# Half tiles moved between full tiles, weight sums moved out of the branches, in an attention and mixture-of-experts kernel

## The chip, the cores and the metric

The kernel runs on one core of a Trainium2 chip, as one launch. The metric is the device time of that launch in microseconds (us). Four engines compute: TensorE (PE in the profile; PEld is its loading of weights), VectorE (DVE), ScalarE (ACT) and GpSimd (POOL). SyncE (SP) only starts transfers. Each engine has its own instruction stream, and a small sequencer of its own (PEldq, DVEq, POOLq in the rows) that handles waits, register loads and branches.

## The reference

```python
# attention, per batch and head: S = 576, D = 64, each row sees itself and the 63 rows before it
scores = where(mask, q @ k.T / sqrt(D), -1e9)
attn = softmax(scores)
x = (attn @ v).transpose(0, 2, 1, 3).reshape(4608, 512)
# experts: 8 of them, every row goes to one
logits = x @ w_gate
expert_idx = argmax(logits, axis=1)
gate_w = softmax(logits)[arange(N), expert_idx]
for e in range(8):                       # rows sorted by expert
    h = maximum(x_sorted[lo:hi] @ w1[e], 0.0)      # 512 -> 1024
    y_sorted[lo:hi] = h @ w2[e]                    # 1024 -> 512
y = gate_w[:, None] * y_sorted[inv_perm]
```

All of it is float32. There are 4608 rows.

## The kernel before, in words

The kernel has three stages. In the first (lines 77 to 400) a scheduler lays out the attention, which writes x to the scratch buffer `x_dram` and collects the routing logits. The second (lines 407 to 530) runs mostly on VectorE: it ranks every row within its expert and turns the rank into a slot, so that `perm_i` holds, for each slot, the row that lies there, and `gate_t` its gate weight. Slots are grouped in tiles of 256 rows (`TB`, two chunks of 128). It also counts, per expert, the chunks in use (`chunks_i`), whether that count is odd (`odds_i`) and the first tile (`starts_i`).

The third stage works on tiles in a hand-written order (`tc.manual_schedule`), expert after expert. A full tile (`body` with `full` true) forms `hidden` and `output` by a scheme with seven products of quarter matrices instead of eight (`x`, `y`, `z`, `w`, and so on are the products), for which sums and differences of the quarters must be formed first: of the rows (`xs`, by `sums_x`), of the hidden values (`hs`, by `left_sums`), and of the weights (`sums_w1`, `sums_w2`, four operations of 128 x 1024 each, on GpSimd). A half tile (an odd last chunk of 128 rows) takes plain products (`plain_hidden`, `plain_output`). In this run there are 19 full tiles and 2 half tiles: three full tiles in three experts, two in five, and a half tile in two of those five.

How many tiles an expert has is known on the chip alone, so each tile stands under a branch: `If(chunks > 1)`, then `If(chunks > 3)` with `If(chunks > 5)` and `If(chunks > 7)` and a loop nested in it, then `If(odds > 0)` for the half tile. A skipped block has a short block in its stead, in which each engine adds to its semaphores what the skipped block would have added; GpSimd also adds it for the skipped indirect transfers.

The order of a tile: `scatter(before)` writes the rows of the tile before to the output with two indirect transfers; GpSimd copies the gate weights; `hidden` runs on the transposed rows `xq`; `turn` transposes the next tile's rows `xg` on TensorE and ScalarE copies them to `xq`; `sums_x` forms `xs` from them on GpSimd; `gather` starts two indirect transfers for the rows of the tile after the next; `output` runs. The first two full tiles of an expert carry an `aside`: at their end GpSimd forms the weight sums of the next expert (`sums_w1` in the first, `sums_w2` in the second; where a tile is skipped, its Else does it). `load_w` starts the transfer of the next expert's weights when the expert begins; two sets of weights are held. All eight experts' counts are loaded into registers of every engine (`values_load`, lines 702 and 703) after the first tile was turned and before the first branch. The last tile's rows are written by a scatter of their own at the end (lines 740 and 741).

`output` keeps five accumulators in half banks of three PSUM tiles `yp`; the product of `hs[:, 2]` adds to the accumulator of `hs[:, 1]`, after VectorE read that one.

## Time and profile before

| what | value |
| --- | --- |
| median of 3 runs (lowest, highest) | 907.71 us (904.1, 911.31) |
| profiled execution | 902.84 us |
| its span, first to last instruction | 901.1 us |
| TensorE busy with matmuls | 790.0 us, 88% of the span |
| VectorE, ScalarE, GpSimd busy | 390.9, 238.1, 371.4 us |
| mean granted TensorE clock | 0.941 of full speed |

The profiled execution lies 1.74 us above its span, and 4.9 us below the median of the three runs. Busy time is a sum over the whole span; the stages have different limits, so the argument goes by stage.

### The profile page before, as it was taken

What the parts mean: (1) busy time and instruction counts of PE and PEld (TensorE: products, weight loads), DVE (VectorE), ACT (ScalarE), POOL (GpSimd) and SP (SyncE); (2) the same over time, 40 slices, a digit from 0 to 9 for tenths busy, and PEclk for the clock granted to TensorE, in tenths of its full rate; (3) what the DMA queues carried; (4) which work ended last, traced back from release to release, by engine and by line L of the source; (5) the groups of instructions that cost most, each with busy time, mean ns of one, the idle gap of its engine ahead of it and who ended that gap; (6) DMA issues with size and microseconds to landing.
All of it is one profiled execution on the core that took longest, in us unless ns stands there. A gap on an engine that the chain in (4) does not pass through costs nothing. (4 is left out here: it accounts for less than half of the span.)

```text
span 901.1 us, 17469 instructions
## 1 busy us (share of the span) xinstructions
PE 790.0 (88%) x6832; PEld 675.9 (75%) x6832; DVE 390.9 (43%) x707; ACT 238.1 (26%) x606; POOL 371.4 (41%) x402
## 2 busy tenths in 40 slices
PE   6999999998931599989979989979989979989991
PEld 5776776776611499979979989969969969979991
DVE  4665665765628025424424432435313424403331
ACT  4554554554500022112211222112202202212220
POOL 3111111415000336635637732675663656663330
PEclk9999999999975799999989998999999989999996
DMA  6668678784080101133151115134134042110101
GB/s 138 153 163 218 147 186 202 197 261 111 3 291 1 35 17 45 47 120 132 48 203 36 36 50 209 47 97 163 43 111 152 34 160 90 49 54 25 48 28 43
DMA packets 140461, 94.46 MB, mean 105 GB/s; under 512 B 118192, under 2 KB 118192, under 8 KB 140338
## 3 DMA queue, kind: packets, MB, share of 16 engines
q1 hardware_dynamic: 128274, 61.90, 24.6%
q0 software_dynamic: 7200, 21.51, 7.2%
q10 hardware_dynamic: 4864, 9.44, 3.0%
q8 instruction: 74, 1.21, 0.6%
q14 instruction: 49, 0.40, 0.1%
HBM read 73.94 MB, written 20.97 MB: 105 GB/s over the span
## 5 line engine op out<-in xcount | busy, mean ns | idle before, releaser
L597 PE MATMUL hp<-xs,s 128*128 128x128 f32 x912 | 111.6, 281 | 0.0
L597 PE MATMUL hp<-xq,w 128*128 128x128 f32 x608 | 84.5, 299 | 28.9 <-PEq L737 23.1
L597 PEld LDWEIGHTS hp<-xs,s 128*128 128x128 f32 x912 | 108.9, 198 | 0.0
L597 PEld LDWEIGHTS hp<-xq,w 128*128 128x128 f32 x608 | 81.5, 213 | 32.7 <-issue 32.1
L629 PE MATMUL yp<-s,hs 128*128 128x256 f32 x456 | 101.5, 379 | 0.0
L284 ACT ACTIVATE pr<-sc,mx 128x128 f32<-128x128 f32 x288 | 79.7, 375 | 66.4 <-DVE mx L281 53.4
L629 PEld LDWEIGHTS yp<-s,hs 128*128 128x128 f32 x456 | 86.6, 190 | 11.8
L120 POOL TENSOR_TENSOR xs<-xq 128x256 f32<-128x256 f32 x44 | 36.9, 839 | 125.7 <-ACT xq L582 125.7
L572 POOL DMA_INDIRECT out_dram<-y,at_s x44 | 44.4, 1009 | 91.8 <-DMA out_dram<-y,at_s 70.1
L120 POOL TENSOR_TENSOR s<-w 128x1024 f32<-128x1024 f32 x32 | 75.3, 2356 | 12.2 <-DMA w<-in_moe_w_dram 12.0
L629 PE MATMUL yp<-w,hq 128*128 128x256 f32 x304 | 71.9, 379 | 0.0
L606 DVE TENSOR_TENSOR part<-hp,part 128x512 f32<-128x512 f32 x19 | 13.1, 692 | 131.3 <-PE hp L597 131.3
L215 POOL COPY vb<-va 64x520 f32<-64x520 f32 x32 | 19.7, 617 | 122.0 <-DMA va<-in_v_dram 70.6
L281 DVE TENSOR_REDUCE mx<-sc 128x3 f32<-128x384 f32 x96 | 49.1, 553 | 41.6 <-PE sc L274 40.2
L636 DVE SCALAR_TENSOR_TENSOR party<-yp,gates,party 128x256 f32<-128x256 f32 x57 | 26.1, 477 | 83.8 <-PE yp L629 83.8
L629 PEld LDWEIGHTS yp<-w,hq 128*128 128x128 f32 x304 | 56.3, 190 | 6.9
L604 ACT COPY part<-hp 128x512 f32<-128x512 f32 x19 | 11.1, 587 | 183.4 <-PE hp L597 183.4
L563 POOL DMA_INDIRECT xg<-x_dram,at_g x46 | 45.5, 989 | 13.6 <-issue 7.0
L293 PEld LDWEIGHTS tr<-ident,pr 128*128 128x128 f32 x288 | 34.4, 144 | 20.1 <-ACT qT L237 8.3
L293 PE MATMUL tr<-ident,pr 128*128 128x128 f32 x288 | 49.3, 286 | 0.1
L653 DVE TENSOR_TENSOR hs<-hq,hs 128x512 f32<-128x512 f32 x19 | 49.0, 2578 | 0.0
L274 PE MATMUL sc<-kT,qT 64*64 64x128 f32 x1152 | 46.5, 285 | 0.2
(137 smaller groups left out, 1379.9 us busy)
## 6 DMA issues: line engine op xcount, KB each, us to landing
w<-in_moe_w_dram SPq DMA_DIRECT2D x16, 2048.0 KB, 11.4
qs<-in_q_dram SPq DMA_DIRECT2D x64, 128.0 KB, 3.1
ks<-in_k_dram SPq DMA_DIRECT2D x64, 128.0 KB, 3.1
va<-in_v_dram SPq DMA_DIRECT2D x64, 128.0 KB, 2.6
x_dram<-xs ACTq DMA_DIRECT2D x8, 1024.0 KB, 5.9
qs<-in_q_dram SPq DMA_DIRECT2D x32, 32.0 KB, 2.5
ks<-in_k_dram SPq DMA_DIRECT2D x32, 32.0 KB, 2.2
vb<-in_v_dram SPq DMA_DIRECT2D x32, 32.0 KB, 2.6
```

Of the source, the lines that this page charges most:

```text
L120: op()
L215: nc.gpsimd.tensor_copy(out=vb[0:D, i].rearrange("p j h d -> p (j h d)"), in_=va[D:P, i].rearrange("p j h d -> p (j h d)"),)
L274: nc.tensor.matmul(out_, lhsT=qT[rows, t, a * WINDOW : (a + 1) * WINDOW], rhs=rhs, start=False, stop=True, skip_group_check=True,)
L281: nc.vector.tensor_reduce(out=mx[:], in_=scs[h][:], axis=AX.X, op=ALU.max, negate=True)
L284: nc.scalar.activation(out=pr[:, m, :], in_=scs[h][:, m, :], func=AF.Exp, bias=mx[:, m : m + 1])
L293: nc.tensor.transpose(out=tr[:, m, :], in_=prs[h][:, m, :], identity=ident[:])
L563: G.indirect_dma_start(out=xg[c][:], out_offset=None, in_=x_dram[:, :], in_offset=bass.IndirectOffsetOnAxis(ap=at_g[:, c : c + 1], axis=0),)
L572: G.indirect_dma_start(out=out[:, :], out_offset=bass.IndirectOffsetOnAxis(ap=at_s[:, c : c + 1], axis=0), in_=ys[c][:], in_offset=None, b ...
L597: nc.tensor.matmul(acc[:, f, :], lhsT=a[:, g, f * P : (f + 1) * P], rhs=b[:, g, :], start=(first and f == 0 and g == 0), stop=(g == HG - 1 ...
L629: nc.tensor.matmul(acc, lhsT=a[:, f, :], rhs=b[:, f, :], start=(first and f == 0), stop=(f == HF - 1), skip_group_check=True,)
L636: onto = lambda out, acc, c, more: V.scalar_tensor_tensor(out=out, in0=acc, scalar=gates[:, c : c + 1], in1=more, op0=ALU.mult, op1=ALU.add)
L653: next(more)()
```

## The change

- The half tile of an expert is worked second, behind its first full tile, and no longer last. For this the slots of the later tiles move up by one tile where an expert has an odd chunk (`late`), `halves_i` holds the tile of the half, and the later tiles stand at `at + odd + t`.
- `sums_w1` of the next expert stands at the start of the expert, ahead of the first branch; `sums_w2` between the first full tile and the branch of the half tile. There is no `aside` and no Else.
- The counts of an expert are loaded by `counts`, one expert ahead, behind `sums_w2` of the expert before it; only those of expert 0 are loaded at the start.
- `sums_x` runs on VectorE, in `output` behind the four sums of `hs`, which now stand together at its head; a half tile has it ahead of `plain_output`.
- `output` uses a sixth half bank (`y2`), so the product of `hs[:, 2]` adds to nothing; VectorE takes one operation more.
- `scatter` stands at the end of its own tile, and the gate weights of the next tile are copied after it. The scatters are declared free of order among themselves. The scatter at the very end is gone.

The diff, cut to its lines:

```diff
@@ -87,7 +87,8 @@
...
-    starts_i = consts.tile([P, E + 1], I32, name="starts_i")
+    starts_i = consts.tile([P, E], I32, name="starts_i")
+    halves_i = consts.tile([P, E], I32, name="halves_i")
@@ -491,12 +492,21 @@
...
+        V.tensor_copy(out=starts_i[:], in_=start[:])
+        V.tensor_single_scalar(halves_i[:], tiles_i[:], 1, op=ALU.min)
+        V.tensor_tensor(out=halves_i[:], in0=halves_i[:], in1=starts_i[:], op=ALU.add)
...
-        V.memset(starts_i[:, 0:1], 0)
-        V.tensor_copy(out=starts_i[:, 1:], in_=cum[:])
+        odd = rt.tile([P, E], F32, name="odd")
+        V.tensor_scalar_mul(odd[:], odds_i[:], float(P))
+        late = rt.tile([P, E, NJ], F32, name="late")
+        V.scalar_tensor_tensor(
+            out=late[:], in0=rank[:], scalar=float(TB + P), in1=per_e(odd, NJ), op0=ALU.is_ge, op1=ALU.mult
+        )
...
+        V.tensor_tensor(out=rank[:], in0=rank[:], in1=late[:], op=ALU.add)
@@ -569,10 +579,12 @@
...
-                G.indirect_dma_start(
+                put = G.indirect_dma_start(
...
+                tc.declare_no_dep(put.ins, group="puts", reason="every token has one slot, so no row is written twice")
+                tc.add_to_no_dep_group("puts", put.ins)
@@ -582,7 +594,7 @@
...
-            form(right_sums(G, xs, xq[:, 0, 0], xq[:, 0, 1], xq[:, 1, 0], xq[:, 1, 1]))
+            form(right_sums(V, xs, xq[:, 0, 0], xq[:, 0, 1], xq[:, 1, 0], xq[:, 1, 1]))
@@ -622,7 +634,6 @@
...
-            more = left_sums(V, hs, a11, a12, a21, a22)
@@ -638,25 +649,24 @@
...
-            x2, w2 = (p[:, hi] for p in yps[0:2])
-            next(more)()
-            next(more)()
+            x2, w2, y2 = (p[:, hi] for p in yps)
+            form(left_sums(V, hs, a11, a12, a21, a22))
...
-            next(more)()
+            sums_x()
...
+            product(y2, hs[:, 2], t[:, 2])
...
-            next(more)()
+            onto(v3[:], y, 1, y1b[:])
+            onto(v3[:], y2, 1, v3[:])
...
-            onto(v2[:], w2, 0, v2[:])
-            product(y, hs[:, 2], t[:, 2], False)
-            onto(v3[:], y, 1, y1b[:])
...
+            onto(v2[:], w2, 0, v2[:])
@@ -683,62 +693,62 @@
...
-        def body(e, before, now, after, full, aside=()):
-            scatter(before)
-            G.tensor_copy(out=gates[:], in_=gate_t[:, now])
+        def body(e, after, now, nxt, full):
...
-            sums_x()
...
-            (output if full else plain_output)(e)
-            for op in aside:
-                op()
+            if full:
+                output(e)
+            else:
+                sums_x()
+                plain_output(e)
+            scatter(now)
+            G.tensor_copy(out=gates[:], in_=gate_t[:, nxt])
+        def counts(e):
+            return (
+                nc.values_load(chunks_i[0:1, e : e + 1], min_val=0, max_val=NT // P),
+                nc.values_load(odds_i[0:1, e : e + 1], min_val=0, max_val=1),
+                G.value_load(starts_i[0:1, e : e + 1], min_val=0, max_val=NTILE),
+            )
+        coming = counts(0)
...
+        G.tensor_copy(out=gates[:], in_=gate_t[:, slice(1, 2)])
...
-        chunks = [nc.values_load(chunks_i[0:1, e : e + 1], min_val=0, max_val=NT // P) for e in range(E)]
-        odds = [nc.values_load(odds_i[0:1, e : e + 1], min_val=0, max_val=1) for e in range(E)]
...
-            at = G.value_load(starts_i[0:1, e : e + 1], min_val=0, max_val=NTILE)
-            if 1 < e + 1 < E:
-                load_w(e + 1)
-            aside = [partial(sums_w1, e + 1), partial(sums_w2, e + 1)] if e + 1 < E else []
+            chunks, odd, at = coming
+            if e + 1 < E:
+                if e:
+                    load_w(e + 1)
+                sums_w1(e + 1)
...
-                return bass.ds(i * C, C), bass.ds(i + 1, 1), bass.ds((i + 3) * C, C)
-            def full(t):
-                body(e, *place(at + t), True, aside[t : t + 1])
-            def otherwise(cond, t):
-                if aside:
-                    with cond.Else():
-                        aside[t]()
-            with tc.If(chunks[e] > 1) as one:
-                full(0)
-            otherwise(one, 0)
-            with tc.If(chunks[e] > 3) as two:
-                full(1)
-                with tc.If(chunks[e] > 5):
-                    full(2)
-                    with tc.If(chunks[e] > 7):
-                        full(3)
+                return bass.ds((i + 3) * C, C), bass.ds((i + 1) * C, C), bass.ds(i + 2, 1)
+            with tc.If(chunks > 1):
+                body(e, *place(at), True)
+            if e + 1 < E:
+                sums_w2(e + 1)
+                coming = counts(e + 1)
+            with tc.If(odd > 0):
+                half = G.value_load(halves_i[0:1, e : e + 1], min_val=0, max_val=NTILE)
+                body(e, *place(half), False)
+            with tc.If(chunks > 3):
+                body(e, *place(at + odd + 1), True)
+                with tc.If(chunks > 5):
+                    body(e, *place(at + odd + 2), True)
+                    with tc.If(chunks > 7):
+                        body(e, *place(at + odd + 3), True)
...
-                            body(e, *place(at + i), True)
-            otherwise(two, 1)
-            with tc.If(odds[e] > 0):
-                nxt = G.value_load(starts_i[0:1, e + 1 : e + 2], min_val=1, max_val=NTILE)
-                body(e, *place(nxt - 1), False)
-        end = G.value_load(starts_i[0:1, E : E + 1], min_val=0, max_val=NTILE)
-        scatter(bass.ds(end * C, C))
+                            body(e, *place(at + odd + i), True)
```

The order in which instructions stand changes at three places of the third stage. The names are the program's: `hp` and `yp` are PSUM tiles of `hidden` and `output`, `s` the weight sums, `party` partial outputs in SBUF.

On TensorE, the end of expert 0's first full tile and what follows it, before:

```order
L629 MATMUL yp_4342<-s_1_4176,hs 128x256 x4
L629 MATMUL yp_4341<-s_1_4176,hs 128x256 x4
L629 MATMUL yp_4342<-s_1_4176,hs 128x256 x4
L629 MATMUL yp_4340<-w_1_4174,hs 128x256 x4
L724 UNCONDITIONAL_BRANCH x2
L727 COMPARE_AND_BRANCH
L597 MATMUL hp_4337<-xq,w_1_4173 128x128 x8
```

and after:

```order
L640 MATMUL yp_4347<-w_1_4175,hs 128x256 x4
L735 UNCONDITIONAL_BRANCH x2
L711 TENSOR_LOAD chunks_i
L712 TENSOR_LOAD odds_i
L740 COMPARE_AND_BRANCH
L679 MATMUL hp_4344<-xq,w_1_4174 128x128 x16
L679 MATMUL hp_4345<-xq,w_1_4174 128x128 x16
L593 MATMUL tp_4342<-ident,xg_4324 128x128 x4
L593 MATMUL tp_4343<-ident,xg_4325 128x128 x4
L691 MATMUL yp_4347<-w_1_4175,hq 128x512 x8
L740 UNCONDITIONAL_BRANCH x2
L743 COMPARE_AND_BRANCH
```

Two register loads and the half tile with its branch now stand between the first and the second full tile; they stood at the start of the stage and behind the nested tiles.

On GpSimd, from the gather of expert 0's first tile to its second tile, before:

```order
L563 DMA xg_4318<-x_dram,at_g 128x512
L120 TENSOR_TENSOR s_1_4175<-w_1_4173 128x1024
L120 TENSOR_TENSOR s_1_4175<-s_1_4175,w_1_4173 128x1024
L120 TENSOR_TENSOR s_1_4175<-w_1_4173 128x1024
L120 TENSOR_TENSOR s_1_4175<-w_1_4173,s_1_4175 128x1024
L724 UNCONDITIONAL_BRANCH
```

and after, from the scatter of the first tile to the branch of the half tile:

```order
L582 DMA out_dram<-y_4338,at_s 4608x512
L707 ISA
L707 COPY gates<-gate_t 128x3
L735 UNCONDITIONAL_BRANCH
L735 ISA
L735 UNCONDITIONAL_BRANCH
L121 TENSOR_TENSOR s_1_4177<-w_1_4175 128x1024
L121 TENSOR_TENSOR s_1_4177<-w_1_4175,s_1_4177 128x1024
L121 TENSOR_TENSOR s_1_4177<-w_1_4175 128x1024
L121 TENSOR_TENSOR s_1_4177<-s_1_4177,w_1_4175 128x1024
L711 TENSOR_LOAD chunks_i
L712 TENSOR_LOAD odds_i
```

The sums of `w1` left the end of the first tile; the sums of `w2` stand there now, behind the tile's own scatter, and the branch of the half tile comes behind them.

On VectorE, one `output`, before:

```order
L618 TENSOR_TENSOR hq<-hp_4339,part_4324 128x512
L642 TENSOR_TENSOR hs<-hq 128x512
L643 TENSOR_TENSOR hs<-hs,hq 128x512
L650 TENSOR_TENSOR hs<-hq 128x512
L636 SCALAR_TENSOR_TENSOR party_4328<-yp_4342,gates,party_4326 128x256
L653 TENSOR_TENSOR hs<-hq,hs 128x512
L636 SCALAR_TENSOR_TENSOR party_4328<-yp_4341,gates,party_4328 128x256
```

and after:

```order
L121 TENSOR_TENSOR hs<-hq 128x512
L121 TENSOR_TENSOR hs<-hs,hq 128x512
L121 TENSOR_TENSOR hs<-hq 128x512
L121 TENSOR_TENSOR hs<-hq,hs 128x512
L121 TENSOR_TENSOR xs<-xq 128x256
L121 TENSOR_TENSOR xs<-xq,xs 128x256
L121 TENSOR_TENSOR xs<-xq 128x256
L121 TENSOR_TENSOR xs<-xs,xq 128x256
L647 SCALAR_TENSOR_TENSOR party_4335<-yp_4349,gates,party_4333 128x256
```

The fourth sum of `hs` stood behind an operation that waits for a product; all four now come first, and the four of `xs` follow.

## Rows read from the trace of the kernel before

**Rows 1.** Stage by stage, the last two stretches (us, busy us per engine, PEclk, DMA):
```profile
314.40:882.90 568.50, 533.94 (x3520) 491.72 (x3520) 212.69 (x286) 106.14 (x198) 300.88 (x288) 0.97 0.24 82
882.90:901.10 18.20, 0.01 (x1) 0.00 (x0) 0.48 (x1) 0.00 (x0) 2.21 (x3) 0.59 0.07 28
```

**Rows 2.** Timeline of TensorE, the transposes of four tiles (start, duration, instruction):
```profile
355.53 1.04 PE L581 MATMUL tp<-ident,xg 128*128 128x128 f32 x8
...
381.69 1.04 PE L581 MATMUL tp<-ident,xg 128*128 128x128 f32 x8
...
844.32 1.04 PE L581 MATMUL tp<-ident,xg 128*128 128x128 f32 x8
...
869.78 1.04 PE L581 MATMUL tp<-ident,xg 128*128 128x128 f32 x8
```

**Rows 3.** Groups from 300 to 902 us (busy, mean ns, idle before, releasers):
```profile
L597 PE MATMUL hp<-xq,w 128*128 128x128 f32 x608 | 84.5, 299 | 28.9 <-PEq L737 23.1 <-issue 5.7
...
L629 PE MATMUL yp<-w,hs 128*128 128x256 f32 x152 | 37.0, 386 | 6.4 <-DVE hs L653 6.4
...
L669 PE MATMUL hp<-xq,w 128*128 128x128 f32 x128 | 16.4, 294 | 5.0 <-PEq L729 5.0
...
L642 DVE TENSOR_TENSOR hs<-hq 128x512 f32<-128x512 f32 x19 | 13.2, 692 | 13.2 <-ACT hq L619 13.2
```

**Rows 4.** Timeline of TensorE at the end of two experts' full tiles:
```profile
392.93 1.89 PE L629 MATMUL yp<-w,hs 128*128 128x256 f32 x8
398.27 0.98 PE L597 MATMUL hp<-xq,w 128*128 128x128 f32 x3 [3.45 <-PEq L737]
...
659.51 2.85 PE L669 MATMUL hp<-xq,w 128*128 128x128 f32 x17 [2.65 <-PEq L729]
```

**Rows 5.** TensorE's sequencer, by line (ns min/median/max, first and last start us):
```profile
L737 PEldq COMPARE_BRANCH  x10: 85/2378/2778, 395.4 to 884.3; - x10
...
L731 PEldq COMPARE_BRANCH  x6: 184/1892/4602, 391.0 to 884.1; - x6
...
L702 PEldq TENSOR_LOAD <-chunks_i x8: 300/306/499, 307.5 to 310.6; - x8
```

**Rows 6.** Ten microseconds behind each restart, first and last of seven (columns of Rows 1):
```profile
398.27:408.27 10.00, 10.00 (x76) 10.00 (x77) 1.38 (x2) 1.18 (x2) 1.47 (x3) 0.85 0.91 326
...
791.38:801.38 10.00, 10.00 (x77) 9.04 (x78) 0.69 (x1) 1.56 (x3) 3.62 (x5) 1.00 0.07 29
```

**Rows 7.** Timeline at the start of the third stage:
```profile
306.36 2.30 PE L581 MATMUL tp<-ident,xg 128*128 128x128 f32 x8 [4.86 <-DMA xg<-x_dram,at_g]
...
314.40 3.77 PE L597 MATMUL hp<-xq,w 128*128 128x128 f32 x16 [5.74 <-issue]
```

**Rows 8.** Timeline in the second tile of expert 0, VectorE beside GpSimd:
```profile
363.99 3.25 DVE L653 TENSOR_TENSOR hs<-hq,hs 128x512 f32<-128x512 f32 x1
364.32 2.36 POOL L120 TENSOR_TENSOR s<-w 128x1024 f32<-128x1024 f32 x1
366.76 2.70 POOL L120 TENSOR_TENSOR s<-w,s 128x1024 f32<-128x1024 f32 x1
```

**Rows 9.** Transfers and GpSimd's sequencer, by line (L137, L572, L737, L765):
```profile
DMA to landing us min/median/max: 8.0/8.7/11.5
...
DMA to landing us min/median/max: 2.1/2.7/8.1
...
L737 POOLq INC_SWDGE_SEM  x6: 482/962/1922, 395.1 to 884.7; - x6
...
L765 POOLq DRAIN  x3: 46/113/8672, 891.5 to 900.8; - x3
```

**Rows 10.** Timeline of the tail:
```profile
883.00 0.48 DVE L636 SCALAR_TENSOR_TENSOR y<-yp,gates,party 128x256 f32<-128x256 f32 x1 [0.32 <-issue]
...
888.77 1.02 POOL L572 DMA_INDIRECT out_dram<-y,at_s  x1 [0.71 <-POOL at_s L569]
891.77 1.00 POOL L572 DMA_INDIRECT out_dram<-y,at_s  x1 [1.97 <-DMA out_dram<-y,at_s]
```

## Prediction

> **What bounds the kernel now.** I read the windows by stage first. From the first hidden product at 314.40 us to 882.90 us TensorE computes in 533.9 of 568.5 us, while VectorE, ScalarE and GpSimd are each busy for little more than half of it or less; behind 882.90 lies a tail of 18.2 us in which hardly anything computes [rows 1]. So the third stage is TensorE's, and the question is what keeps TensorE from 34.6 us of work in it, what slows it, and what the start and the tail cost. The first stage keeps its order, so I take it as unchanged.
>
> The timeline gives a full tile's price without trouble: the transposes of two tiles in a row near the end, where no weight sums are formed any more, stand 25.46 us apart; in expert 0 they stand 26.16 us apart [rows 2]. The groups by line say who is waited for [rows 3]: 28.9 us ahead of the first products of `hidden`, 23.1 of them put down to TensorE's own sequencer at the branch of the half tile (L737) and 5.7 to the first start; 5.0 us ahead of a half tile, put down to the sequencer at L729; and 6.4 us ahead of products that wait for the fourth sum of `hs`. So 23.1 + 5.0 = 28.1 us fall at seven ends of a run of full tiles. One of them shows the pattern: the array ends at 394.82 and starts at 398.27, 3.45 us later; ahead of a half tile it is 2.65 us [rows 4], ahead of the other half tile 5.0 - 2.65 = 2.35. The sequencer's list says why [rows 5]: a branch over a block takes 2.4 us in the median at L737 and up to 4.6 us at L731. The first at L731 starts at 391.0, thus 3.8 us before the array ends. The sequencer runs that far ahead, so the first jump of an expert's end is mostly covered and the second isn't.
>
> The clock follows. [...] The sum of what is missing is 1.33 windows, 13.3 us. The one window with 1.00 stands behind the shortest gap, 2.35 us; the others follow 2.65 us and more.
>
> **The change part by part**, against the profiled execution of 902.84 us; the median of the runs, 907.71, lies 4.9 us above it, and I carry that over.
>
> *Start.* Sixteen register loads (two lists of eight, 0.44 us from one to the next [rows 5]) stand between the end of the transposes at 308.66 and the first product, 5.74 us [rows 7]. After, two loads of 0.3 us stand ahead of the transposes, beside their wait for the gather. The routing gains `odd`, `late` and a sum ahead of the slots: three operations that the trace lacks; at most 0.48 us each, as an operation of 128x256 takes [rows 10], and little over nothing for fewer columns. I take the dear end, since small operations pay mostly their start: 5.7 - 1.4 = **-4.3** (bounds -3 to -5.5).
>
> *Skips.* At an expert's end only the skip over the nested tiles is left, since the half tile's stands earlier; 2.4 to 4.6 us against a lead of 3.8 leaves 0 to 0.8. TensorE's next products also wait for the short blocks of the others, VectorE's above all, whose last operation ends 0.5 us behind the array. I take 1.0 at seven ends (0.85 to 1.6), and 0.9 once in the last expert. Behind the first full tile of the six experts without a half tile the sequencer has two loads and a jump: 0.9 + 2.4 to 4.6 - 3.8 = -0.5 to 1.7. VectorE's chain there is 0.48 + two loads of 0.3 + some 0.3 for its block, 1.4. I take 1.4 at five of them (up to 2.4; the sixth is the last expert's). The two experts with a half tile fall through. Sum 7.0 + 0.9 + 7.0 = 14.9 in place of 28.1: **-13.2** (bounds -16 to -4).
>
> *Clock.* All these gaps are below 2.35, behind which the clock stayed at 1.00, so the loss of **-13.3** goes. If the five behind first tiles come out at 2.65 or more, each pays what such a restart pays now, 13.3 / 6 = 2.2 us: -2.3 is the other bound.
>
> [...]
>
> *The fourth sum of `hs`.* In fourteen tiles it waits for an operation that waits for a product, and meets GpSimd's weight sums: 3.25 us where VectorE's like takes 0.69 [rows 3, 8]. Those tiles cost 26.16 - 25.46 = 0.70 us more: 14 x 0.70 = **-9.8**. With all four at the head nothing stands before them.
>
> *What GpSimd's sums meet now.* The sums of `w1` start when the weights land, 8.0 to 8.7 us after their issue at the expert's start [rows 9], and take four times some 2.4 us [rows 8]; they end some 18 us into the first tile, while the four sums of `hs` stand from 14 to 17 us and the second is wanted at about 19. That overlap did not exist before. If VectorE's four take 3.25 instead of 0.69 each, they end at 27 and the products wait some 2 us in each of six experts, or 11 us in all; if they meet only the last sum, nothing. I take 1.0 us in all (**+1.0**, bounds 0 to 11), as the second sum, which is wanted first, has some 3 us of slack, one operation of 3.25.
>
> *Sums of `w2` on GpSimd's queue.* They begin behind the first tile's scatter, and the short block for the skipped half tile stands behind them in GpSimd's queue. The scatter's two issues, of 1.0 us each [rows 10], lie about 1.4 to 3.7 us behind the tile's end; four sums of 2.4 us end at some 13.2 us, and the block's additions for skipped transfers take 0.5 to 1.9 us [rows 9]. Waiting for them is `turn` of the second tile, 14 us in. So it waits 0 to 1.4 us in five experts; I take 0.85 each: **+4.3** (bounds 0 to 7).
>
> *`xs` on VectorE, the sixth half bank.* Four sums of half the width of those of `hs` and one more operation of 0.48 us cost VectorE about 2 us in a tile of 25.5, in which it is busy for 10; they lie behind the sums that TensorE waits for. `xs` is wanted a tile later. Nothing on the path. Should VectorE run late, the next tile's first products would wait; I see no row for that.
>
> *Tail.* Now the last operation of `y` ends at 883.5, and the last scatter is issued at 888.77 and 891.77, the second behind a wait of 1.97 us; then GpSimd drains for up to 8.7 us [rows 9, 10]. After, the scatter stands in the tile, ahead of the closing branches, so some 4.5 us earlier, but its drain has the skipped blocks in front of it still. I take **-4.0** (bounds -1 to -6.6: the whole of 888.77 - 883.5 and the half of the wait that is not the first transfer's).
>
> **Sum**: -4.3 - 13.2 - 13.3 - 9.8 + 1.0 + 4.3 - 4.0 = -39.3. The profiled execution comes to 863.5, the median to 907.7 - 39.3 = **868 us**.
>
> **The rivals.** *The lead is lost behind the first tile.* It needs the sequencer to be 3.8 us ahead; a wait late in `output` would take that away. Then five gaps cost 3.8 in place of 1.4 and 2.2 of clock: 5 x 4.6 = +23, 891 us. For it speaks that the second of two jumps is uncovered now; against it, that the first is covered.
>
> *Slower: every skip is paid in idle array.* There are twelve of them (seven ends, five first tiles), where now seven gaps hold all. With a gap x and a clock loss of 2.2 at each, the sum gains 12 (x + 2.2) - 14.9: at 4.6 us, the longest jump, +66.7, thus 935 us. It breaks even at x = 2.3 us (908 us), and as the clock held behind 2.35 us, a gap just above that is where it decides. For it: skips that stood in pairs now stand alone, each with loads or waits before it. Against it: the lead of 3.8 at the end of a full tile [rows 4, 5] covers most of a single skip.
>
> [...] A sum of `hs` begun at 363.99 ended at 367.24, though GpSimd's sum began later, at 364.32 [rows 8]; so VectorE loses whichever begins first. If all sums of `hs` wait for the last of `w1`, the term of 1.0 becomes 11: 878 us. [...]
>
> *The change removes nothing.* That the idle time only moves is the break-even of the second rival, 908.
>
> **How the numbers follow.** The sum as it stands 0.72, the port 0.06, the lead lost at first tiles 0.10, every skip paid 0.12, of which 0.07 near the break-even and 0.05 above. One per cent, 9 us, is about what a measurement of this kernel tells from no change. So faster 0.88, same 0.07, slower 0.05. The sum's own bounds, with not all at one end, are 855 to 885; to hold 8 in 10 the range reaches to the lost lead: 855 to 892.
>
> **What would show it.** Idle time of TensorE behind first full tiles and at experts' ends near 1 to 1.4 us, and the clock at 1.00 behind them; transposes of full tiles 25.5 us apart with no wait for the fourth sum of `hs`; at second tiles a wait of `turn` for GpSimd of at most 1.4 us; the first hidden product near 310; a tail of some 14 us. I am wrong if gaps of 2.4 us and more stand at more than seven places, if `hs` of first tiles takes 3 us an operation and is waited for, or if `turn` waits for GpSimd for several microseconds.

## The result, and the profile after

The changed kernel takes 875.85 us (median of 4 runs, 875.18 to 876.66); the kernel before, beside it, 906.35 us (904.1 to 911.31). The ratio is 0.966, with an interval of 0.961 to 0.970: 30.5 us less, where 39.3 were forecast, and inside the range. The profiled execution has a span of 874.8 us, 26.3 us less than the span before.

The start, on TensorE's timeline of the changed kernel (start, duration, instruction, idle time before it):

```profile
311.47 1.08 PE L593 MATMUL tp<-ident,xg 128*128 128x128 f32 x4 [4.92 <-DMA xg<-x_dram,at_g]
...
313.77 3.62 PE L609 MATMUL hp<-xq,w 128*128 128x128 f32 x16
```

The first product stands 2.3 us behind the first transpose, before it was 8.0 [rows 7]; the 5.74 us of idle time are gone. Yet it starts only 0.6 us earlier, since the transposes start 5.1 us later. The copy that ends the first stage shows why, in VectorE's timeline of the kernel before and of the changed one:

```profile
256.44 0.23 DVE L367 COPY logits<-tr 128x72 f32<-128x72 f32 x1 [1.96 <-PE tr L363]
```

```profile
260.46 0.23 DVE L368 COPY logits<-tr 128x72 f32<-128x72 f32 x1 [1.96 <-PE tr L364]
```

So 4.0 us of the 5.1 were there before the routing began, in a stage whose instructions stand in the same order in both kernels. Most of that agrees with a lower granted clock: in windows of 15 us over the first 255 us, 5.1 us of full clock are missing in the profile before and 8.7 us in this one. The other 1.1 us are the routing's new operations, among them two of 128x288, 0.46 us each, and one of 128x8, 0.16 us: with 8 columns for 288 an operation still takes a third of the time.

What TensorE waits for in the third stage of the changed kernel (engine, line and releaser: us in all, times, the longest):

```profile
PE hp L609 <- DVEq L740: 6.4, 5, 1.4
PE yp L640 <- DVE hs L121: 4.7, 8, 0.8
PE hp L609 <- DVEq L745: 3.4, 4, 0.9
PE hp L609 <- issue: 2.5, 1, 2.5
PE tp L593 <- DMA xg<-x_dram,at_g: 2.0, 4, 1.0
PE hp L609 <- DVEq L747: 1.6, 2, 0.8
```

Against [rows 3] the 23.1 and 5.0 us put down to TensorE's own sequencer have gone. In their place stand gaps of 1.4 us behind first full tiles (L740 and, for one that ends at 343.58, 1.5; in the last expert, which loads no counts, 0.7) and of 0.8 to 0.9 at experts' ends (L745, L747), which VectorE's sequencer ends; with one of 2.5 us at an expert's end they come to 15.4 us at thirteen places, where there were 28.1 at seven. The wait for `hs` is a new one: not for the fourth sum, but in first tiles, for the earlier ones. The transposes' wait behind GpSimd, which the prediction has, is there with 2.0 us.

Windows of ten microseconds behind an expert's end and behind a first tile, and the tail (us, busy us per engine, granted clock of TensorE, DMA):

```profile
395.66:405.66 10.00, 10.00 (x89) 10.00 (x90) 2.08 (x3) 1.25 (x3) 2.22 (x3) 1.00 0.97 339
685.45:695.45 10.00, 10.00 (x89) 10.00 (x90) 2.08 (x3) 1.26 (x3) 9.62 (x7) 1.00 0.14 55
858.65:874.80 16.15, 0.00 (x0) 0.00 (x0) 0.48 (x1) 0.00 (x0) 2.22 (x3) 0.66 0.08 31
```

The granted clock is 1.00 in the ten microseconds behind each of the thirteen restarts; behind the same expert's end it was 0.85 before [rows 6]. Before, the five windows between the first and the last of [rows 6] lay below 1.00, too:

```profile
457.60:467.60 10.00, 10.00 (x67) 10.00 (x68) 0.81 (x2) 1.18 (x2) 1.21 (x2) 0.74 0.89 307
541.92:551.92 10.00, 10.00 (x63) 10.00 (x64) 0.69 (x1) 1.18 (x2) 1.46 (x3) 0.69 0.90 323
602.67:612.67 10.00, 10.00 (x75) 10.00 (x76) 1.38 (x2) 1.18 (x2) 1.21 (x2) 0.83 0.91 321
659.51:669.51 10.00, 10.00 (x73) 9.91 (x74) 0.69 (x1) 0.90 (x2) 4.34 (x5) 0.83 0.06 26
733.90:743.90 10.00, 10.00 (x67) 10.00 (x68) 0.72 (x2) 1.18 (x2) 1.21 (x2) 0.73 0.90 322
```

The tail is 2.0 us shorter, not 4.0.

A tile without weight sums beside `hs` has its price of 25.5 us: expert 0's second tile lies between these transposes, 25.49 us apart, where it took 26.16 before [rows 2].

```profile
356.22 1.06 PE L593 MATMUL tp<-ident,xg 128*128 128x128 f32 x8
...
381.71 1.04 PE L593 MATMUL tp<-ident,xg 128*128 128x128 f32 x8
```

First tiles of later experts are longer. The worst, on TensorE, and VectorE and GpSimd in it:

```profile
668.90 1.04 PE L593 MATMUL tp<-ident,xg 128*128 128x128 f32 x8
...
675.84 1.99 PE L640 MATMUL yp<-s,hs 128*128 128x256 f32 x8 [0.72 <-DVE hs L121]
678.60 3.72 PE L640 MATMUL yp<-s,hs 128*128 128x256 f32 x16 [0.76 <-DVE hs L121]
...
685.45 2.02 PE L609 MATMUL hp<-xq,w 128*128 128x128 f32 x16 [1.40 <-DVEq L740]
...
699.15 1.06 PE L593 MATMUL tp<-ident,xg 128*128 128x128 f32 x8 [0.97 <-DMA xg<-x_dram,at_g]
```

```profile
670.49 2.54 DVE L121 TENSOR_TENSOR hs<-hq 128x512 f32<-128x512 f32 x1 [0.69 <-ACT hq L631]
673.07 2.72 DVE L121 TENSOR_TENSOR hs<-hs,hq 128x512 f32<-128x512 f32 x1
675.71 2.83 DVE L121 TENSOR_TENSOR hs<-hq 128x512 f32<-128x512 f32 x1
678.47 0.68 DVE L121 TENSOR_TENSOR hs<-hq,hs 128x512 f32<-128x512 f32 x1
```

```profile
667.69 2.36 POOL L121 TENSOR_TENSOR s<-w 128x1024 f32<-128x1024 f32 x1 [8.25 <-DMA out_dram<-y,at_s]
...
672.43 2.80 POOL L121 TENSOR_TENSOR s<-w 128x1024 f32<-128x1024 f32 x1
675.20 2.79 POOL L121 TENSOR_TENSOR s<-w,s 128x1024 f32<-128x1024 f32 x1
```

Three of the four sums of `hs` take the time of a GpSimd sum each; only the last, behind GpSimd's end, takes 0.68 us. From transpose to transpose (668.90 to 699.15) it is 30.25 us; without the gap of 1.40 and the transposes' wait of 0.97 it is 27.88.

### The profile page after: what moved, and what is told of

It reads as the page before. It is cut to its first block, busy times and chain, and to the rows that moved or that the text cites. A ratio compares the mean times of both kernels' runs of the same rounds, so it can differ in the third digit from the quotient of the medians.

```text
span 874.8 us, 17497 instructions
## 1 busy us (share of the span) xinstructions
PE 780.4 (89%) x6832; PEld 664.8 (76%) x6832; DVE 430.0 (49%) x818; ACT 237.7 (27%) x606; POOL 307.7 (35%) x312
## 5 line engine op out<-in xcount | busy, mean ns | idle before, releaser
L609 PE MATMUL hp<-xs,s 128*128 128x128 f32 x912 | 108.4, 276 | 0.5 <-DVE part L618 0.5
L640 PE MATMUL yp<-s,hs 128*128 128x256 f32 x456 | 103.4, 381 | 4.7 <-DVE hs L121 4.7
L609 PEld LDWEIGHTS hp<-xs,s 128*128 128x128 f32 x912 | 105.3, 193 | 0.7 <-DVE part L618 0.7
L121 POOL TENSOR_TENSOR s<-w 128x1024 f32<-128x1024 f32 x32 | 78.3, 2449 | 57.2 <-DMA out_dram<-y,at_s 38.3
L609 PE MATMUL hp<-xq,w 128*128 128x128 f32 x608 | 76.6, 280 | 15.4 <-DVEq L740 7.9
L609 PEld LDWEIGHTS hp<-xq,w 128*128 128x128 f32 x608 | 73.0, 196 | 21.2 <-issue 21.0
L573 POOL DMA_INDIRECT xg<-x_dram,at_g x46 | 50.3, 1094 | 79.4 <-PE tp L593 69.1
L647 DVE SCALAR_TENSOR_TENSOR party<-yp,gates,party 128x256 f32<-128x256 f32 x76 | 34.9, 479 | 57.4 <-PE yp L640 56.2
L121 DVE TENSOR_TENSOR hs<-hq 128x512 f32<-128x512 f32 x38 | 45.2, 1190 | 13.2 <-ACT hq L631 13.2
L275 PEld LDWEIGHTS sc<-kT,qT 64*64 64x64 f32 x1152 | 33.9, 138 | 12.6 <-issue 8.6
```

The lines of the kernel that those rows point to most:

```text
L121: op()
L275: nc.tensor.matmul(out_, lhsT=qT[rows, t, a * WINDOW : (a + 1) * WINDOW], rhs=rhs, start=False, stop=True, skip_group_check=True,)
L573: G.indirect_dma_start(out=xg[c][:], out_offset=None, in_=x_dram[:, :], in_offset=bass.IndirectOffsetOnAxis(ap=at_g[:, c : c + 1], axis=0),)
L609: nc.tensor.matmul(acc[:, f, :], lhsT=a[:, g, f * P : (f + 1) * P], rhs=b[:, g, :], start=(first and f == 0 and g == 0), stop=(g == HG - 1 ...
L640: nc.tensor.matmul(acc, lhsT=a[:, f, :], rhs=b[:, f, :], start=(first and f == 0), stop=(f == HF - 1), skip_group_check=True,)
L647: onto = lambda out, acc, c, more: V.scalar_tensor_tensor(out=out, in0=acc, scalar=gates[:, c : c + 1], in1=more, op0=ALU.mult, op1=ALU.add)
```

## The experiments

Each changes one thing in the changed kernel (875.85 us) unless it says otherwise. They were timed in three groups, beside which the kernel before took 905.05, 908.15 and 907.83 us, so differences between groups of 2 us or less say little; the traces say more. The ratios are to the kernel before.

**The sums of w1 left out.** The sums of `w1` are formed for the second expert only.

```diff
-                sums_w1(e + 1)
+                if not e:
+                    sums_w1(e + 1)
```

> The changed kernel, but GpSimd forms the sums of w1 for the second expert only; experts 3 to 8 then work with old sums, so that part of the computation is left out. Theory A: in the first tiles of experts 2 to 7 the sums of hs take up to 2.8 us each beside these sums, and that costs the 7.5 us by which those tiles are longer than 25.7; with five of these six left undisturbed (the sums for expert 2 stand in the first expert's tile, where none was lengthened), the hs sums take 0.7 us, the idle time ahead of the products of hs (4.7 us) goes to nothing, and the time falls by 6 to 7.5 us to about 869. Theory B: these tiles are longer because the weight transfer or the restart after the branch makes the sums late; then the time stays within 1.5 us of 876 and the hs sums stay long.

Measured: 870.57 us (869.13 to 871.2), ratio 0.962 [0.958, 0.965]. (All six lengthened tiles were left undisturbed, not five, as the expectation has it.) VectorE's second sum of `hs` in the same tile as above, and TensorE there:

```profile
667.18 0.69 DVE L121 TENSOR_TENSOR hs<-hs,hq 128x512 f32<-128x512 f32 x1
```

```profile
664.87 1.04 PE L593 MATMUL tp<-ident,xg 128*128 128x128 f32 x8
...
679.39 2.02 PE L609 MATMUL hp<-xq,w 128*128 128x128 f32 x16 [1.40 <-DVEq L741]
...
693.12 1.07 PE L593 MATMUL tp<-ident,xg 128*128 128x128 f32 x8 [0.99 <-DMA xg<-x_dram,at_g]
```

The sums take 0.69 us, no product of `hs` waits, and the tile takes 28.25 - 1.40 - 0.99 = 25.86 us, 2.0 less. Theory A holds: GpSimd's sums of `w1` cost this, not the restart or the transfer. Over the six experts the same difference, tile by tile, comes to 7.2 us. The medians differ by 5.3; in the profiled execution one restart, at 581.97, loses clock (0.83 over ten microseconds, 1.7 us), which may be the rest.

**The sums of w1 in the first tile, behind its gather.**

```diff
             gather(after)
+            if aside:
+                aside()
...
-                sums_w1(e + 1)
...
+            if aside:
+                with one.Else():
+                    aside()
```

> The changed kernel with the sums of w1 back in the expert's first tile, behind its gather (an Else forms them where that tile is skipped). Theory A: the sums of hs run while GpSimd waits for the gather's turn, so at most the last of them meets a sum of w1; the 7.5 us in first tiles go. But GpSimd ends these sums 1 to 2 us behind the tile's end, so the sums of w2 and the short block end later, and the second tile's transposes wait 0.5 to 1 us more in five experts: in all 870 to 872 us. Theory B (the first tiles are long for another reason): 876 to 880.

Measured: 897.37 us (896.33 to 898.32), ratio 0.991 [0.988, 0.995], 21 us slower than the changed kernel and outside of both theories. TensorE's waits, VectorE behind `hs`, and TensorE's restart:

```profile
PE hp L609 <- DVEq L745: 28.9, 6, 5.7
```

```profile
417.94 2.57 DVE L121 TENSOR_TENSOR xs<-xq 128x256 f32<-128x256 f32 x1
```

```profile
429.99 2.26 PE L609 MATMUL hp<-xq,w 128*128 128x128 f32 x9 [5.64 <-DVEq L745]
```

No product waits for `hs` any more, but now it is `xs` that stands beside GpSimd's sums: three of its four operations take 2.5 us, for 0.42 elsewhere. VectorE ends its tile 4 us later, reaches its two branches later, and TensorE's gap behind the first tile grows from 1.4 to 5.6 us, with a lower clock behind it. That `xs` costs nothing, as the prediction had it, held in these runs only where GpSimd formed no sum beside it (0.42 us an operation).

**The sums of w2 behind the half tile's branch.**

```diff
-                sums_w2(e + 1)
                 coming = counts(e + 1)
...
+            if e + 1 < E:
+                sums_w2(e + 1)
             with tc.If(chunks > 3):
```

> The changed kernel with the sums of w2 behind the half tile's branch, not ahead of it. Theory A: the second tile's transposes wait (0.17 to 0.97 us, 2.0 us in all) because GpSimd's additions in the short block of the skipped half tile stand behind the sums of w2; with these behind the branch the waits go: -2.0 us, about 874. Rival: what they wait for is the rows' gather itself, or the sums that now stand closer to the second tile make its gather late: 876 or some us more.

Measured: 874.56 us (873.22 to 875.57), ratio 0.965 [0.962, 0.969]. The transposes that waited 0.97 us before them in the changed kernel, in this run's timeline:

```profile
698.31 1.04 PE L593 MATMUL tp<-ident,xg 128*128 128x128 f32 x8
```

No transpose of the third stage waits any more. In time it is 1.3 us, no more than groups differ by; the trace shows theory A's wait gone.

**The half tile last again.**

```diff
-        V.tensor_tensor(out=rank[:], in0=rank[:], in1=late[:], op=ALU.add)
...
+                            body(e, *place(at + i), True)
             with tc.If(odd > 0):
                 half = G.value_load(halves_i[0:1, e : e + 1], min_val=0, max_val=NTILE)
```

> The changed kernel with the half tile last in its expert again (slots and branch order as before, all else as changed). Theory A: the place of the half tile is what splits the pair of skips; with it back at the end, seven ends have gaps of 2.4 to 5.3 us again, those behind first tiles fall to 1 us or less, and behind each gap of 2.65 us or more the clock falls again: 28 us of gaps for 15 and some 13 us of clock, so about 893 to 902 us. Rival: the gaps became short because GpSimd's sums and the register loads moved; then 874 to 880 us and no window of the third stage below a clock of 1.00.

Measured: 881.41 us (878.74 to 883.36), ratio 0.973 [0.969, 0.977]. TensorE's largest wait, one window behind an expert's end, and the tail:

```profile
PE hp L601 <- PEq L741: 13.9, 4, 3.7
```

```profile
395.61:405.61 10.00, 10.00 (x75) 10.00 (x76) 1.38 (x2) 1.18 (x2) 0.63 (x2) 0.83 0.92 334
```

```profile
860.56:880.20 19.64, 0.00 (x1) 0.00 (x0) 0.48 (x1) 0.00 (x0) 2.22 (x3) 0.57 0.07 26
```

The pair of skips is back at four ends, 3.3 to 3.7 us each, but no gap is over 3.7 where the kernel before had three over 5.2, and the gaps ahead of half tiles, 2.4 and 2.6 us before, are 0.8 now. Behind first tiles there is none. So 5.6 us, not 17 to 26: both theories were off. In the trace the gaps come to 17.8 us for 15.4, so the place of the half tile bears little of what the skips gained. It bears more of the clock: behind five restarts the windows are at 0.71 to 0.83 and miss 9.7 us. The tail takes 3.5 us more. Against these stand waits that shrink, for `hs` from 4.7 to 1.3 us and of the transposes from 2.0 us to none. Something else had made the remaining skips shorter; the next run shows what.

**The fourth sum of hs late again.**

```diff
-            form(left_sums(V, hs, a11, a12, a21, a22))
+            more = left_sums(V, hs, a11, a12, a21, a22)
+            for _ in range(3):
+                next(more)()
...
             onto(v2[:], y, 0, y1a[:])
+            next(more)()
```

> The changed kernel with the fourth sum of hs behind the first operation on the accumulators again, all else as changed. Theory A, as the prediction had it: its place behind a wait is what cost 0.70 us in fourteen tiles, so some 10 us come back, 884 to 887 us. Theory B: the loss came from GpSimd's sums standing beside it, which the change moved to the start of the first two tiles; then the sum takes 0.7 us, TensorE doesn't wait for it, and the time stays at 875 to 877. Theory C: TensorE doesn't wait, but its sequencer has the last products' wait later and loses part of its lead, so that the gaps at the ends of experts grow from 0.8 us to 2 us or more, with a lower clock behind some: 880 to 890.

Measured: 887.86 us (886.34 to 889.65), ratio 0.982 [0.974, 0.990]. TensorE's waits that changed, and two restarts:

```profile
PE hp L609 <- PEq L748: 9.1, 4, 2.4
...
PE hp L609 <- PEq L750: 4.6, 2, 2.4
```

```profile
452.05 3.65 PE L609 MATMUL hp<-xq,w 128*128 128x128 f32 x16 [2.27 <-PEq L748]
```

```profile
534.98 2.02 PE L609 MATMUL hp<-xq,w 128*128 128x128 f32 x16 [2.39 <-PEq L750]
```

Here is the other part. No tile waits for the fourth sum: it takes 0.68 us where GpSimd is quiet. But all seven gaps at experts' ends grow, six from 0.8 or 0.9 to 2.2 to 2.4 us and one from 2.5 to 4.6, and the releaser is TensorE's own sequencer again at six of them. The kernel before shows at the end of its second expert what the jump waits for: the last products stood behind the fourth sum, which ended at 450.17, and the jump began at 450.3.

```profile
446.92 3.25 DVE L653 TENSOR_TENSOR hs<-hq,hs 128x512 f32<-128x512 f32 x1
...
450.31 1.97 PE L629 MATMUL yp<-w,hs 128*128 128x256 f32 x8 [0.45 <-DVE hs L653]
```

```profile
L729 PEldq COMPARE_BRANCH  x1: 3703/3703/3703, 450.3 to 450.3; - x1
```

So there the sequencer passed the last products' wait before it went ahead to the branch, and I read this run the same way, with a wait that ends late. The jump over the nested tiles of expert 0, in the changed kernel and then in this run (ns min/median/max, first and last start us):

```profile
L747 PEldq COMPARE_BRANCH  x1: 3702/3702/3702, 390.8 to 390.8; - x1
```

```profile
L750 PEldq COMPARE_BRANCH  x2: 179/1804/3429, 391.1 to 394.9; - x2
```

The array ends at 394.84 in the changed kernel and at 393.15 here, so the jump begins 4.0 us ahead of that end there and 2.1 us ahead of it here. The same lead, 4.0 and 2.1 us, stands at all thirteen restarts of the two traces; a jump of 3.3 to 3.8 us is covered by the first and not by the second. Theory C holds: the head position of the four sums gives the sequencer its lead. The size in the forecast (10 us) was right for a reason that was only half of it.

**All counts at the start.**

```diff
-        coming = counts(0)
+        known = [counts(e) for e in range(E)]
...
-                coming = counts(e + 1)
```

> The changed kernel with the counts of all experts loaded at the start again. Theory A: the loads stand ahead of the transposes on every engine, GpSimd's 24 ahead of the first gather; so the first product comes some 8 to 10 us later, less what the wait for the gather hides, and behind the six first tiles the gap of 1.4 us loses its two loads on VectorE (0.6 us each, 3.6 us in all). Sum +2 to +6, 878 to 882 us. Theory B: the gaps behind first tiles don't hang on VectorE's loads and stay at 1.4: 882 to 886.

Measured: 875.0 us (872.13 to 875.76), ratio 0.966 [0.958, 0.974]: no difference that could be told. The start, and what TensorE waits for:

```profile
310.00 1.08 PE L593 MATMUL tp<-ident,xg 128*128 128x128 f32 x4 [4.90 <-DMA xg<-x_dram,at_g]
...
312.37 2.98 PE L609 MATMUL hp<-xq,w 128*128 128x128 f32 x13
```

```profile
PE hp L609 <- DVEq L739: 6.5, 6, 2.2
PE tp L593 <- DMA xg<-x_dram,at_g: 4.8, 5, 1.6
```

Both theories expected a later start, and there is none: sixteen loads ahead of the transposes are covered as well as two, and the first product stands 2.4 us behind the first transpose, for 2.3 in the changed kernel. It was their place, behind the transposes, that cost 5.7 us before. The gaps behind first tiles shrink from 7.9 us to 6.5, and the transposes' wait grows by 2.8: what is won at the gap seems to be waited for behind GpSimd's sums of `w2`, on which that wait hung above; this run alone doesn't show it.

**Two and five register loads more on VectorE** behind the first tile (five: `range(5)`).

```diff
+                for _ in range(2):
+                    V.value_load(chunks_i[0:1, e : e + 1], min_val=0, max_val=NT // P)
                 coming = counts(e + 1)
```

> The changed kernel with two register loads more on VectorE between the first tile and the half tile's branch. Theory A: TensorE's gap there ends with VectorE's short block, so six gaps of 1.4 us (and the one of 0.7) grow by 0.3 to 0.45 us per load, to 2.0 to 2.3; that is no more than the 2.37 us behind which the clock stayed at 1.00, so the clock holds: +4 to +6, 880 to 882 us. Theory B: TensorE's own sequencer sets the gap; then nothing changes, 875 to 877.

> The changed kernel with five register loads more on VectorE at the same place. Theory A: the gaps grow to 2.9 to 3.6 us, beyond 2.65; each then pays the gap and some 2.2 us of lower clock, so 6 times 1.5 to 2.2 plus 13: +22 to +26, 898 to 902 us, with windows below 1.00 behind first tiles. If the clock doesn't fall behind such gaps: 885 to 889. Theory B (TensorE's own sequencer sets the gap): 875 to 877.

Measured: 887.7 us (885.06 to 888.48), ratio 0.980 [0.973, 0.988], and 902.91 us (901.49 to 908.05), ratio 0.997 [0.993, 1.000]. TensorE's waits with two, and with five, and a restart with five (423.50 with 1.41 us in the changed kernel):

```profile
PE hp L609 <- DVEq L742: 15.2, 6, 3.2
```

```profile
PE hp L609 <- DVEq L742: 27.3, 6, 5.5
```

```profile
431.34 3.64 PE L609 MATMUL hp<-xq,w 128*128 128x128 f32 x16 [5.17 <-DVEq L742]
```

TensorE's gap behind a first tile hangs on VectorE's sequencer, load by load: in the five experts that load counts there it grows from 1.4 or 1.5 us to 2.7 to 3.2 with two loads and to 5.2 to 5.5 with five, some 0.7 to 0.9 us a load, twice what was expected. With two loads the clock, too, was below 1.00 behind four of the five gaps, so theory A's 880 to 882 us were missed; with five its 898 to 902 came within 1 us. The sixteen products behind the gap of 5.17 take 3.64 us where they take 2.02 at full clock. Five gaps of over 5 us and the clock behind them eat nearly the whole gain: that is what the slower rival feared, idle array and lost clock at each place, here at five of its twelve.

**Two sums of w1 ahead of the tile, two behind its gather**, and the sums of w2 behind the half tile's branch; then the same **with all counts at the start**.

```diff
-                sums_w1(e + 1)
+                first, rest = parts_w1(e + 1)
+                form(first)
...
             gather(after)
+            if aside:
+                aside()
...
-                sums_w2(e + 1)
...
+                sums_w2(e + 1)
             with tc.If(chunks > 3):
```

> The changed kernel with two of the four sums of w1 ahead of the first tile's branch, two in the tile behind its gather, and the sums of w2 behind the half tile's branch. Theory: what VectorE loses it loses where a sum of its own stands beside one of GpSimd's, be it hs (the changed kernel) or xs (the run with all four sums in the tile); with the gather of 3 us on GpSimd while hs is formed, only the first of hs and two of xs meet a sum, some 2 us each, and the chain behind xs starts no later than in the changed kernel. So the hs waits (6 to 7.5 us) and the transposes' waits (2 us) go with the gaps unchanged: 866 to 869 us. Rival: two met sums of xs already make VectorE's last operation late; gaps of 3 us and more behind first tiles and 880 us or more.

> As the run with the split sums of w1, and all counts are loaded at the start, ahead of the first gather. Theory: loading there costs nothing (the first product stood 2.4 us behind the transposes' start with it too) and takes 0.6 us from each of six gaps; what the changed kernel gave back in the transposes' waits is gone, since the sums of w2 stand behind the branch. So 3 to 4 us less than the split alone, 863 to 866 us. Rival: something else waits up to the same point, and both runs take the same within 1 us.

Measured: 877.71 us (876.83 to 879.76), ratio 0.968 [0.965, 0.971], and 873.13 us (872.39 to 873.42), ratio 0.962 [0.959, 0.966]. TensorE's waits of the first and of the second, and VectorE and GpSimd in one tile of the second:

```profile
PE hp L613 <- DVEq L750: 13.5, 6, 3.4
```

```profile
PE hp L613 <- DVEq L748: 10.0, 6, 2.7
```

```profile
672.83 5.43 DVE L121 TENSOR_TENSOR xs<-xq 128x256 f32<-128x256 f32 x1
```

```profile
673.30 2.36 POOL L121 TENSOR_TENSOR s<-w 128x1024 f32<-128x1024 f32 x1
675.61 2.36 POOL L121 TENSOR_TENSOR s<-w,s 128x1024 f32<-128x1024 f32 x1
```

The waits for `hs` and of the transposes are gone, as the theory had it, and the gaps behind first tiles grew, as the rival had it: one sum of `xs`, begun at 672.83, ends at 678.26, behind both sums of GpSimd that begin after it. The 866 to 869 us were missed, and so were the 863 to 866 of the second run. With the counts at the start the gaps are 3.5 us shorter. By its median this is the fastest kernel here that leaves nothing out, 2.7 us below the changed one, but the two come from different groups, and their ratios to the kernel before overlap.

**The kernel before with the four sums of hs at the head alone**, and **with the half tile second alone** (slots moved as in the change).

```diff
-            next(more)()
-            next(more)()
+            form(left_sums(V, hs, a11, a12, a21, a22))
```

```diff
+            with tc.If(odds[e] > 0):
+                half = G.value_load(halves_i[0:1, e : e + 1], min_val=0, max_val=NTILE)
+                body(e, *place(half), False)
             with tc.If(chunks[e] > 3) as two:
```

> The kernel before with one part of the change alone: all four sums of hs at the head of output. Theory A: the late fourth sum cost 0.7 us in fourteen tiles and TensorE's sequencer its lead at their ends; the gaps of 5.3 us fall to 3.3 and those of 2.4 to 2.7 ahead of half tiles below 1.5, with less lost clock behind them: 10 us of waits, 11 of gaps and some 5 of clock, so 880 to 890 us. Theory B: at the head the sums meet GpSimd's sums of xs and the weights' instead; the products of hs wait there, and the time is 898 to 910.

> The kernel before with another part alone: the half tile second in its expert, with the slots moved for it; sums, loads and scatter as before. Theory A: the place of the half tile by itself parts the pair of skips, and the gaps and the clock behind them fall as in the changed kernel: 15 to 25 us less than before, 882 to 892. Theory B: it needs the sequencer's lead, which the late fourth sum of hs takes away behind the first tile and at the ends of two-tile experts; then gaps of 2.4 us and more stand at both places, and the time is 900 to 915.

Measured: 895.27 us (890.37 to 896.24), ratio 0.987 [0.983, 0.990], and 905.58 us (900.46 to 908.41), ratio 0.997 [0.995, 0.999]. TensorE's waits of the first, then of the second:

```profile
PE hp L597 <- PEq L733: 21.6, 5, 4.4
```

```profile
PE hp L607 <- PEq L742: 12.7, 5, 2.7
PE hp L607 <- POOLq L737: 9.9, 5, 2.1
```

The head alone takes away the tiles' waits and the gaps over 5 us: 12.6 us, less than theory A's 18 to 28, since gaps of 4.1 to 4.5 us stay: two jumps stand there, of 4.2 to 4.6 and 2.8 to 2.9 us, and the lead is 4.0. The half tile alone brings next to nothing, theory B: the largest gaps at ends fall to 2.7 us, but GpSimd's short block stands behind the sums of the aside and holds the second tile's products for 2.1 us (POOLq), and the wait for the fourth sum stays at 6.3 us. At five of its seven ends the lead is 1.9 us, as in the kernel before. So at the ends the two parts need one another: one jump instead of two, and a lead of 4.0 us to cover it. How much they bring together without the rest of the change was not run; alone they bring 12.6 and 2.3 us of 30.5, and taking them out of the changed kernel costs 12.0 and 5.6.

## Why the prediction was right, and where it was off

The terms against the two traces, in us; the first is the time from the end of the first stage to the first product, the second the sum of the gaps, and so on:

| term | forecast | traces |
| --- | --- | --- |
| start | -4.3 | -5.7 + 1.1 = -4.6 |
| skips | -13.2 | 15.4 - 28.1 = -12.7 |
| clock | -13.3 | -13.3 |
| fourth sum of `hs` | -9.8 | -9.8 |
| sums of `w1` beside `hs` | +1.0 | +7.2 |
| sums of `w2` on GpSimd | +4.3 | +2.0 |
| tail | -4.0 | -2.0 |
| not assigned | 0 | some +3 |
| first stage | 0 | +4.0 |

**The mechanism was right in the main**: the gain lies in the skips, the clock behind them, the fourth sum and the start, and each is within 0.5 us of its term. Behind first tiles the gap is the 1.4 us of VectorE's chain that the prediction worked out. The term of the clock is what the seven windows of before miss to 1.00 (0.15, 0.26, 0.31, 0.17, 0.17, 0.27 and 0 of ten microseconds, 1.33 windows or 13.3 us). Without the first stage's 4.0 us the spans differ by 30.3 us, close to the medians' 30.5.

**One step was right by luck.** The prediction took a lead of 3.8 us for every end from the one that it shows. In the trace of before the sequencer has 3.8 us at two of the seven ends, those behind three full tiles, and 1.9 us at the other five, where the late fourth sum holds it back (until 450.17 in the rows with the run of the late fourth sum); that is why three gaps were over 5 us. The 3.8 us came true, as 4.0 at all ends, because the four sums moved to the head, which the prediction had not counted under the skips.

**The step that was mis-sized** is the overlap of the sums of `w1` with `hs`, "I take 1.0 us in all", argued from a slack of 3 us, "one operation of 3.25". Three sums of `hs` in a row meet a sum of GpSimd, not one; the second ends at 675.79 instead of 671.9 (3.0 us behind the transposes' start, as in the run without these sums), and the products that want them follow one another, so that each adds a wait. Part of it is when GpSimd starts. The prediction had the sums begin when the weights land, 8.0 to 8.7 us after their issue, and end 18 us into the tile. In this expert the weights, issued at 655.70, land 10.0 us later, but the first sum begins at 667.69, 12.0 us after the issue: GpSimd's block for the skipped tiles stands ahead of it and waits for the landing of the last tile's scatter, which now is issued at the tile's end (656.91, landing 8.5 us later). The sums end 20.0 to 21.7 us into the six tiles. That was the third rival, which the chances call the port, with its 11 us: 7.2 of them came. No run shows a port; what they show is how long VectorE's sums take. The time, 875.85, lies nearer to its 878 than to 868, though the tail and the unassigned 3 us have a part in that. It had been given a chance of 0.06, too little for a case that the trace of before already showed in [rows 8].

VectorE is held in every tile shown here in which its sums of `hs` or `xs` stand beside GpSimd's sums of the weights: 3.25 us for 0.69 in the kernel before [rows 3, 8], 2.5 to 2.8 for 0.68 in the changed kernel's first tiles, 2.5 for 0.42 in the run with all four sums in the tile. Which engine begins first doesn't settle by how much. In the first tiles above VectorE's sums begin behind GpSimd's and the two take turns; in the run with the split sums and all counts at the start the sum of `xs` begun at 672.83, ahead of GpSimd's, ended behind two of them, begun at 673.30 and 675.61, 5.43 us for 0.42.

**The tail** gained 2.0 for 4.0: the last issue of the scatter stands 2.7 us behind the array's end, where it stood 8.9, but GpSimd's block for the skipped tiles stands between it and the end, as said, and takes 4.2 us, from 862.37 to 866.6. Its additions for the skipped transfers alone are 1.9 us of that, from 864.2. The drain behind it then takes 7.35 us; before, 7.4 us passed from the end of the last issue to the drain's end [rows 9, 10]. With the half tile last the tail is 3.5 us longer, which no term had.

**Reasons that did not hold, though the size did.** The prediction named two reasons for the start, fewer loads and their place ahead of the transposes; the place alone does it (the run with all counts at the start). For the fourth sum's wait, too, it named two, the place behind another wait and the sums of the weights beside it, and gave the gain to the place; taking away either is enough (the runs with the fourth sum late and with the head alone). What the place at the head is worth in the changed kernel is the sequencer's lead at the ends of experts (seven gaps there grew by 1.4 to 2.2 us, 11 us in all), which the prediction had put down to the place of the half tile alone. And the clock is not decided by the gap's length as I had it, below.

Why a jump takes 3.3 to 3.8 us at the experts' ends of the changed kernel, no row shows. The change removed no skip and yet 12.7 of the 28.1 us of idle time at them went: what counts in these runs is whether the sequencer reaches the branch early enough while the array still works. With a lead of 4.0 us the jumps left gaps of 0.8 to 0.9 us at six of the seven ends, with one of 2.1 us gaps of 2.2 to 2.4 (the run with the fourth sum late).

**What stays open**: why the clock was lower in the first stage. Its copy of the logits stands at 256.4, 257.7 and 258.6 us in the three profiles with the code of before in it and at 258.9 to 260.9 in the eleven others; whether that is chance or has a cause was not tried. Open are also the 3 us without a place, of which some 1.2 may be six more restarts (a tile with one takes 25.7 us without its gap in the changed kernel, and 25.5 without one), and the one gap of 2.5 us ahead of 589.11, for which the trace names no releaser.

## What to carry to other kernels

At a branch, set the length of the jump against the lead that the engine's sequencer has, at every such place and not at one: at the end of expert 0 a jump of 3.4 us against a lead of 2.1 left 2.2 us of idle time, and one of 3.7 against a lead of 4.0 left 0.8, which VectorE's sequencer, later still, ended. Then look for the last wait that the sequencer passes before the branch: the fourth sum of `hs`, moved ahead of such a wait, was worth 12.0 us in the changed kernel, 11 of them in the gaps at experts' ends. When work is moved to another time on one engine, lay its new time beside every operation of the engine that it slows: here each new place of GpSimd's sums met something of VectorE's, first `hs` (2.5 to 2.8 us a sum for 0.68), then `xs` (2.5 and 5.43 for 0.42). And undo the parts one by one, in the old kernel and in the new: the half tile's place brought 2.3 us alone and cost 5.6 when it was taken out of the changed kernel.

## What the runs showed of the hardware

The granted clock does not follow from the gap ahead alone. Behind 2.27 us it fell (sixteen products in 3.65 us, against 2.02), behind 2.39 us in the same execution it did not (both rows stand with the run of the late fourth sum), and in the run with all counts at the start it held behind a gap of 3.12 us (1.00 over the ten microseconds behind it):

```profile
586.98 1.94 PE L609 MATMUL hp<-xq,w 128*128 128x128 f32 x16 [3.12 <-issue]
```

So the prediction's reading, that gaps below 2.35 us keep the clock, fails at 2.27. What else decides was not tried.

In the run with the split sums and all counts at the start one VectorE sum of `xs` was held by two GpSimd sums in a row (5.43 us for 0.42), while in the changed kernel's first tiles the two engines took turns, 2.5 to 2.8 us each.
